# An RWKV-6 recurrence with a gated feed-forward behind it: x of one superblock transposed by DMA, products moved to GpSimd, and a new order

## The chip, the core and the metric

One NeuronCore of a Trainium2 chip runs the whole kernel. Its engines work side by side, each through a queue of its own in order: TensorE (PE; PEld is its weight loading), VectorE (DVE), ScalarE (ACT), GpSimd (POOL) and SyncE (SP), which here only issues transfers. An instruction waits at the head of its queue until the semaphores that it needs have come, and what stands behind it waits too. PE writes its results to PSUM; the other data lie in SBUF.

The metric is the device time of one execution in microseconds (us). Three runs of the kernel before gave 204.59, 204.86 and 205.42; the median is 204.86.

## The reference, cut to what matters

```python
def _attn_ref(r, k, v, w, u):              # batch 4, heads 8, positions 768, head size 48
    for t in range(S):
        cur = einsum('bhd,bhe->bhde', u[None] * kt, vt)
        y[:, :, t] = einsum('bhd,bhde->bhe', rt, state + cur)
        state = wt[:, :, :, None] * state + einsum('bhd,bhe->bhde', kt, vt)

def _moe_ref(x, w_gate, w_val, w_out, rms_g):   # 3072 rows of 384, inner size 1536
    xn = x / sqrt(mean(x * x, axis=-1) + 1e-06) * rms_g
    g = xn @ w_gate
    return (g * (1.0 / (1.0 + exp(-g))) * (xn @ w_val)) @ w_out
```

The first function carries a state of 48 x 48 for each batch and head along the positions. Its output, with the heads side by side, is the x of the second.

## The kernel before, in words

The 768 positions are cut into six superblocks n = 0 to 5 of 128 positions, and each holds the four batches j = 0 to 3. For one (n, j) the recurrence is done in chunk form:

- `load_k`, `load_r`, `load_v`, `load_w` fetch the inputs (SP). `ln` takes the logarithm of w (ACT); `cs_mm` sums it along the positions on PE; `cs_add` makes k's sums out of r's on DVE; `exp_r` and `exp_k` are the exponentials (ACT).
- `r_mul` (L438) and `k_mul` (L444) multiply r and k with them into `rk`. For (n, j) in `EXPR_SB` the exponential of r's sums is written to a tile `er` in SBUF, else over the sums in PSUM. `K_POOL` lists the k products that GpSimd computes; it reads SBUF, so their exponential is written to `ek`.
- `rk` is transposed: for superblocks 0 and 1 on PE (`rk_pe`, L467) with a copy on ACT (`rk_tr`, L476), from 2 on by a DMA transpose (`rk_tr`, L472).
- `q_mm` forms the scores (L485, L487), `q_mask_e`, `q_copy_o` and `q_mask_o` (L503, an affine select on POOL) mask them, `y_mm` (L530, L533) gives the output. `st_mm` (L513) and `st_new` bring the state on.
- `bonus_mul` (two POOL products, L450 and L451), `bonus_sum` and `bonus_v` make the term with u; `x_add` adds it.
- `x_sq` and `x_rstd` give the scale of each row, `xn_mul` (L556) applies it. x is then transposed into `xnt[n]`: for superblocks 0 to 3 on PE (`xn_pe`, L567) and copied out by DVE with the factor rms_g (`xn_out`, L578); for 4 and 5 by a DMA transpose (`xn_tr`, L561), and DVE multiplies rms_g in afterwards (`xn_gain`, L582) in three pieces of 128 features, each over all 512 rows.

The feed-forward of a superblock has 12 gate blocks and 12 value blocks of three matmuls (`gate_mm`, `val_mm`, L593), each followed by `silu` on ACT or `h_mul` on DVE, and four output blocks of 12 matmuls (`o_mm`, L625). A block needs all four batches of `xnt[n]`. `load_gv` and `load_wo` fetch the weights, and POOL issues them (L344, L350): a small and a large piece of each of w_gate and w_val (columns 0 to 511 and 512 to 1535), and three pieces of w_out.

Which step comes when is written out by hand in the string `ORDER`; every engine's queue takes its part of it in that order. So the feed-forward of superblock n is interleaved with the recurrence of n + 1. `warm` is a matmul whose result nobody reads. PSUM has eight banks in three rings: two for r's sums and gate blocks ("a"), two for k's sums and value blocks ("b"), four for the rest ("q").

The lines of the recurrence's two products and of the gain, and how a step is called:

```python
nc.vector.tensor_tensor(out=rk[:, n % 2, j, 0, :, 0:D], in0=inp["r", n, j],
                        in1=bank["cs_r", n, j][:, NP:NP + DM]..., op=ALU.mult)
eng = nc.gpsimd if (n, j) in K_POOL else nc.vector
for step in ORDER.split():
    fn, n, j = step.split(".")
    fns[fn](int(n), int(j))
```

Of the kernel before, what the change touches and what calls it, by code (L numbers as in the profile page):

```python
# [12 lines left out]
ALU = mybir.AluOpType  # L13
# [22 lines left out]
cast_v.0.2 cs_mm.1.0 exp_r.1.0 exp_k.1.0 bonus_sum.0.2 q_mask_o.0.0 q_mm.0.1 q_mask_e.0.1 q_mask_o.0.1 bonus_mul.0.3
bonus_sum.0.3 bonus_v.0.0 rk_pe.0.3 rk_tr.0.3 cs_mm.1.1 exp_k.1.1 exp_r.1.1 cast_v.0.3 load_v.2.1 load_k.2.1 load_r.2.3
load_r.2.2 load_k.2.0 warm.14.0 y_mm.0.0 warm.19.0 x_add.0.0 warm.3.0 x_sq.0.0 cast_v.1.0 q_mm.0.2 q_mask_e.0.2
q_mask_o.0.2 x_rstd.0.0 xn_mul.0.0 q_mm.0.3 y_mm.0.1 warm.35.0 x_add.0.1 warm.34.0 x_sq.0.1 x_rstd.0.1 load_v.2.0
q_mask_e.0.3 w_tot.0.3 load_gv.0.0 y_mm.0.2 bonus_v.0.2 x_add.0.2 x_sq.0.2 st_mm.0.3 cs_mm.1.3 xn_mul.0.1 x_rstd.0.2  # L40
load_k.2.2 q_mask_o.0.3 y_mm.0.3 w_tot.1.0 k_mul.1.0 bonus_v.0.3 x_add.0.3 x_sq.0.3 r_mul.1.0 st_mm.0.2 xn_pe.0.1
xn_out.0.1 xn_pe.0.0 load_gv.0.1 xn_out.0.0 st_new.0.3 cs_mm.1.2 xn_mul.0.2 xn_pe.0.2 st_mm.0.1 xn_out.0.2 st_new.0.1
x_rstd.0.3 xn_mul.0.3 xn_pe.0.3 xn_out.0.3 bonus_mul.1.0 load_gv.1.0 exp_r.1.3 exp_k.1.2 exp_r.1.2 rk_pe.1.0 rk_tr.1.0
r_mul.1.1 st_mm.1.0 st_new.1.0 w_tot.1.1 bonus_sum.1.0 bonus_mul.1.1 exp_k.1.3 gate_mm.0.1 gate_mm.0.0 silu.0.1
q_mm.1.0 q_mask_e.1.0 w_tot.1.3 val_mm.0.0 val_mm.0.1 k_mul.1.1 rk_pe.1.1 st_new.0.2 silu.0.0 h_mul.0.0 r_mul.1.3
rk_tr.1.1 gate_mm.0.3 silu.0.3 h_mul.0.1 load_gv.1.1 bonus_v.1.0 gate_mm.0.2 silu.0.2 q_copy_o.1.0 val_mm.0.2
gate_mm.0.4 silu.0.4 val_mm.0.3 q_mm.1.1 h_mul.0.2 gate_mm.0.6 silu.0.6 q_copy_o.1.1 k_mul.1.3 h_mul.0.3 q_mask_o.1.0
w_tot.1.2 y_mm.1.0 x_add.1.0 gate_mm.0.8 rk_pe.1.3 gate_mm.0.5 q_mask_e.1.1 bonus_sum.1.1 silu.0.8 val_mm.0.4 h_mul.0.4
k_mul.1.2 r_mul.1.2 bonus_mul.1.3 x_sq.1.0 rk_tr.1.3 silu.0.5 gate_mm.0.11 val_mm.0.5 val_mm.0.9 h_mul.0.5 q_mask_o.1.1
gate_mm.0.9 cast_v.1.1 st_mm.1.1 st_new.1.1 silu.0.9 h_mul.0.9 rk_pe.1.2 rk_tr.1.2 val_mm.0.6 h_mul.0.6 gate_mm.0.7  # L50
q_mm.1.2 q_mask_e.1.2 silu.0.11 q_copy_o.1.2 q_mm.1.3 q_mask_e.1.3 load_wo.1.0 x_rstd.1.0 load_wo.0.0 val_mm.0.11
h_mul.0.11 q_copy_o.1.3 val_mm.0.8 h_mul.0.8 load_wo.2.0 bonus_v.1.1 silu.0.7 xn_mul.1.0 y_mm.1.1 x_add.1.1
gate_mm.0.10 silu.0.10 x_sq.1.1 bonus_sum.1.3 val_mm.0.7 h_mul.0.7 val_mm.0.10 h_mul.0.10 o_mm.0.0 bonus_mul.1.2
bonus_sum.1.2 o_out.0.0 bonus_v.1.3 cast_v.1.3 q_mask_o.1.3 y_mm.1.3 x_add.1.3 ln.2.0 cs_mm.2.0 cs_add.2.0 q_mask_o.1.2
cast_v.1.2 y_mm.1.2 xn_pe.1.0 xn_out.1.0 st_mm.1.3 ln.2.1 cs_mm.2.1 x_rstd.1.1 xn_mul.1.1 exp_k.2.0 exp_r.2.0
bonus_v.1.2 x_add.1.2 x_sq.1.2 x_sq.1.3 load_v.2.2 x_rstd.1.2 cs_add.2.1 exp_r.2.1 w_tot.2.0 st_new.1.3 ln.2.2 o_mm.0.1
ln.2.3 x_rstd.1.3 xn_mul.1.3 st_mm.1.2 st_new.1.2 xn_mul.1.2 w_tot.2.1 r_mul.2.0 o_out.0.1 cast_v.2.1 bonus_mul.2.1
# [75 lines left out]
def kernel(  # L133
# [41 lines left out]
    def sel(s):  # L175
        return {(int(x[0]), int(x[1])) for x in s.split()}
# [501 lines left out]
```

## Time and profile before

| What | Value |
|---|---|
| median of three runs | 204.86 us |
| the profiled execution's own time | 204.97 us |
| span, first to last instruction | 203.3 us |
| mean granted clock of TensorE | 0.999 |
| transfers | 32.41 MB, mean 159 GB/s |

A row of the timeline gives start, duration, engine, line of the kernel, operation, output and inputs, shape and count; in brackets the idle time before it and what ended that. A row of a group gives count, total busy time, mean duration in ns, idle time before and its causes. In the rows of windows the busy time of PE, PEld, DVE, ACT and POOL follows the length. A row of issues ends with the median time from issue to landing.

### The profile page before, as it was taken

To read this page: it belongs to the slowest core of one execution; us is meant where nothing else is said; L and a number is where in the kernel's file an instruction comes from. 1 tells how busy PE (TensorE), PEld (TensorE's weight loads), DVE (VectorE), ACT (ScalarE), POOL (GpSimd) and SP (SyncE) were. 2 spreads that over 40 slices of the span, in tenths; PEclk is the share of its full clock that TensorE was granted. 3 is DMA by queue.
4 is the path that set the end of the run, shared out by engine and by line. 5 is a ranking of instruction groups with operands and counts; after the bars stand their busy time and mean duration, and the time that the engine had idled before them with its cause. 6 is when DMAs were issued, how large, how long until landed. Compare 5 with 4: busy or idle time off the path is not lost.

```text
span 203.3 us, 4409 instructions
## 1 busy us (share of the span) xinstructions
PE 189.9 (93%) x1569; PEld 113.1 (56%) x1588; DVE 154.2 (76%) x299; ACT 137.7 (68%) x278; POOL 125.4 (62%) x186
## 2 busy tenths in 40 slices
PE   1999879998999999999999999999969999999994
PEld 1566555554666555665556665555635565555562
DVE  6158999889899879997899998687996685145621
ACT  2379999767899647998659886688975666154300
POOL 6079983592659968999978789776895543000000
PEclk9999999999999999999999999999999999999999
DMA  6998999999986999995999999997155201121012
GB/s 156 266 224 177 187 220 208 212 175 215 203 172 141 204 161 206 248 234 128 204 171 221 241 215 207 221 194 165 44 141 159 61 23 40 58 77 42 0 64 92
DMA packets 121566, 32.41 MB, mean 159 GB/s; under 512 B 116420, under 2 KB 120392, under 8 KB 121544
## 3 DMA queue, kind: packets, MB, share of 16 engines
q1 hardware_dynamic: 119504, 28.58, 66.1%
q0 software_dynamic: 2032, 3.54, 9.6%
q8 instruction: 12, 0.20, 0.4%
q14 instruction: 10, 0.08, 0.1%
q10 hardware_dynamic: 8, 0.00, 0.0%
HBM read 25.96 MB, written 4.72 MB: 151 GB/s over the span
## 4 chain that ended last, share of the span: by engine, by line
PE 84%; ACT 6%; DVE 3%; issue 2%; POOL 1%; DMA 1%; POOLq 0%; DVEq 0%
PE ps_bv L593 12%; PE ps_au L593 12%; PE ps_av L593 10%; PE ps_bu L593 10%; PE ps_qu L625 7%; PE ps_qx L625 5%; PE ps_qv L625 4%; PE ps_qz L625 4%; PE ps_qx L367 1%; DVE rk L438 1%; ACT xn L556 1%; ACT junk L543 1%; DMA xnt<-xn 1%; PE ps_qv L485 1%; PE ps_qu L467 1%
## 5 line engine op out<-in xcount | busy, mean ns | idle before, releaser
L625 PEld LDWEIGHTS <-ht 128*128 128x128 bf16 x300 | 28.4, 98 | 17.0
L593 PEld LDWEIGHTS <-wv_sb 128*128 128x128 bf16 x216 | 23.2, 114 | 21.2 <-issue 1.5
L230 ACT ACTIVATE sg<-ps_au 128x512 bf16<-128x512 f32 x38 | 22.8, 599 | 17.4 <-PE ps_au L593 13.9
L593 PEld LDWEIGHTS <-wg_sb 128*128 128x128 bf16 x216 | 23.1, 114 | 18.9 <-issue 0.2
L611 DVE TENSOR_TENSOR ht<-ps_bv,sg 128x512 bf16<-128x512 f32 x38 | 26.1, 688 | 9.3 <-PE ps_bv L593 5.1
L230 ACT ACTIVATE sg<-ps_av 128x512 bf16<-128x512 f32 x34 | 20.4, 600 | 16.1 <-PE ps_av L593 9.7
L593 PE MATMUL ps_bv<-xnt,wv_sb 128*128 128x512 bf16 x110 | 30.7, 380 | 0.3
L593 PE MATMUL ps_au<-xnt,wg_sb 128*128 128x512 bf16 x110 | 30.5, 380 | 0.4
L611 DVE TENSOR_TENSOR ht<-ps_bu,sg 128x512 bf16<-128x512 f32 x34 | 23.3, 686 | 9.2 <-ACT sg L230 6.0
L450 POOL TENSOR_TENSOR ruk<-rt,kt 128x384 f32<-128x384 f32 x24 | 24.6, 1023 | 7.8 <-DMA rt<-in_r_dram 7.0
L593 PE MATMUL ps_bu<-xnt,wv_sb 128*128 128x512 bf16 x94 | 27.1, 380 | 2.0 <-DVE xnt L582 1.5
L460 POOL TENSOR_TENSOR ydiag<-vt,diag 128x384 f32<-128x384 f32 x24 | 20.1, 840 | 12.1 <-DVE diag L455 12.0
L593 PE MATMUL ps_av<-xnt,wg_sb 128*128 128x512 bf16 x99 | 27.3, 380 | 0.1
L451 POOL TENSOR_TENSOR ruk<-ruk,u_bc 128x384 f32<-128x384 f32 x24 | 24.2, 1009 | 1.9
L503 POOL TENSOR_SCALAR_AFFINE_SELECT qts<-qts 128x512 bf16<-128x512 bf16 x20 | 12.6, 637 | 8.8 <-ACT qts L496 7.3
L556 ACT ACTIVATE xn<-xb,rstd 128x384 bf16<-128x384 f32 x24 | 14.5, 611 | 4.5 <-POOL rstd L552 4.3
L625 PE MATMUL ps_qu<-wo_sb,ht 128*128 128x384 bf16 x96 | 16.9, 326 | 0.0
L444 POOL TENSOR_TENSOR rk<-kt,ek 128x384 bf16<-128x384 f32 x16 | 15.9, 1001 | 1.1 <-ACT ek L230 1.1
L228 ACT ACT_TABLE_LOAD x10 | 12.8, 1283 | 1.8 <-PEq L662 1.6
L543 ACT ACTIVATE junk<-xb 128x384 bf16<-128x384 f32 x24 | 12.4, 518 | 1.3 <-DVE xb L538 1.1
L230 ACT ACTIVATE lw<-wt 128x384 bf16<-128x384 f32 (+1 forms) x20 | 11.0, 578 | 2.8 <-DMA wt<-in_w_dram 2.7
L455 DVE TENSOR_REDUCE diag<-ruk 128x8 f32<-128x384 f32 x24 | 12.8, 545 | 0.0
(156 smaller groups left out, 370.8 us busy)
## 6 DMA issues: line engine op xcount, KB each, us to landing
kt<-in_k_dram SPq DMA_DIRECT2D x24, 192.0 KB, 3.6
vt<-in_v_dram SPq DMA_DIRECT2D x24, 192.0 KB, 4.1
rt<-in_r_dram SPq DMA_DIRECT2D x24, 192.0 KB, 3.9
out_dram<-ob SPq DMA_DIRECT2D x23, 192.0 KB, 2.8
wt<-in_w_dram SPq DMA_DIRECT2D x16, 192.0 KB, 3.6
wt<-in_w_dram SPq DMA_DIRECT2D x4, 384.0 KB, 4.4
wo_sb<-in_moe_w_out_dram POOLq DMA_DIRECT2D x3, 384.0 KB, 7.1
wg_sb<-in_moe_w_gate_dram POOLq DMA_DIRECT2D x1, 768.0 KB, 9.4
```

Of the source, the lines that this page charges most:

```text
L228: nc.scalar.preload_act_table_set(table_name)
L230: return nc.scalar.activation(**kw).ins
L444: eng.tensor_tensor(out=rk[:, n % 2, j, 1, :, 0:D], in0=inp["k", n, j], in1=bank["cs_k", n, j][:, 0:DM].rearrange("p (h d) -> p h d", h=H) ...
L450: nc.gpsimd.tensor_tensor(out=ruk[n, j], in0=inp["r", n, j], in1=inp["k", n, j], op=ALU.mult)
L451: nc.gpsimd.tensor_tensor(out=ruk[n, j], in0=ruk[n, j], in1=u_bc, op=ALU.mult)
L455: nc.vector.tensor_reduce(out=diag[n, j].rearrange("p h o -> p (h o)"), in_=ruk[n, j], axis=mybir.AxisListType.X, op=ALU.add)
L460: nc.gpsimd.tensor_tensor(out=ydiag[n, j], in0=inp["v", n, j], in1=diag[n, j].to_broadcast([128, H, D]), op=ALU.mult)
L543: nc.scalar.activation(out=junk, in_=xb[n, j], func=AF.Square, accum_out=rstd[n, j][:, 0:1])
L556: nc.scalar.activation(out=xn, in_=xb[n, j], func=AF.Copy, scale=rstd[n, j][:, 1:2])
L593: nc.tensor.matmul(ps, lhsT=units(ws, c, f), rhs=xnt[n][:, c, :], start=(c == 0), stop=(c == KC - 1))
L611: nc.vector.tensor_tensor(out=ht[n][:, f, :], in0=bank.pop(("v", n, f)), in1=bank.pop(("sg", n, f)), op=ALU.mult)
L625: nc.tensor.matmul(ps[:, cols], lhsT=ht[n][:, f, b * L:(b + 1) * L], rhs=wo_sb[:, f, cols], start=(f == 0), stop=(f == FC - 1))
```

## The change

The transposes of x of superblock 3 move from PE to DMA. For superblocks 3 to 5 rms_g is multiplied in on GpSimd, in four pieces (one for each batch, all 384 features) instead of DVE's three. k's products of superblock 1 move from DVE to GpSimd. The exponential of r's sums of superblock 1 stays in PSUM. The warm matmuls read a tile `zero` of their own, 128 x 128, and there are 48 of them and not 36. `ORDER` is a new one throughout; the parts below are those up to the first block of the feed-forward, the end of superblock 2's feed-forward and the end of superblock 3's.

```diff
 ORDER = """
...
+load_k.0.0 load_w.0.1 warm.18.0 warm.5.0 warm.17.0 load_w.0.0 load_r.0.2 warm.10.0 warm.36.0 warm.21.0 ln.0.1 warm.1.0
+warm.14.0 load_r.0.0 bonus_mul.0.0 bonus_sum.0.0 load_w.0.3 load_v.0.0 load_w.0.2 load_k.0.1 load_r.0.1 bonus_mul.0.1
+ln.0.0 cs_mm.0.0 warm.33.0 load_v.0.1 load_k.0.2 bonus_mul.0.2 cs_mm.0.1 warm.11.0 warm.24.0 warm.26.0 warm.37.0
+warm.25.0 warm.29.0 warm.2.0 warm.19.0 load_k.0.3 load_r.0.3 exp_r.0.0 w_tot.0.0 r_mul.0.0 load_v.0.2 load_r.1.1
+load_v.1.0 load_r.1.0 load_k.1.0 load_v.0.3 load_k.1.1 load_r.1.3 load_r.1.2 load_k.1.3 exp_r.0.1 exp_k.0.0 k_mul.0.0
...
+xn_pe.0.1 xn_out.0.1 xn_mul.0.2 xn_pe.0.2 warm.45.0 xn_out.0.2 x_rstd.0.3 xn_mul.0.3 xn_pe.0.3 xn_out.0.3 rk_pe.1.1
+rk_tr.1.0 bonus_sum.1.0 bonus_v.1.0 bonus_mul.1.3 exp_r.1.2 r_mul.1.2 w_tot.1.3 st_mm.1.0 exp_k.1.2 q_mm.1.0
+q_copy_o.1.0 q_mask_o.1.0 bonus_mul.1.1 k_mul.1.2 val_mm.0.3 val_mm.0.1 w_tot.1.2 gate_mm.0.1 silu.0.1 st_new.1.0
...
+y_mm.3.2 x_add.3.2 val_mm.2.9 h_mul.2.9 h_mul.2.11 ln.4.0 cs_mm.4.0 ln.4.1 cs_mm.4.1 cs_add.4.1 bonus_mul.4.1
+cs_add.4.0 x_sq.3.1 x_rstd.3.1 x_sq.3.2 x_sq.3.3 x_rstd.3.3 o_mm.2.2 o_out.2.2 o_mm.2.1 xn_mul.3.1 xn_tr.3.1 exp_r.4.1
+w_tot.4.1 o_mm.2.0 st_new.3.3 bonus_sum.4.1 r_mul.4.1 exp_r.4.0 w_tot.4.0 r_mul.4.0 xn_mul.3.3 xn_tr.3.3 ln.4.3
+cs_mm.4.3 xn_gain.3.0 x_rstd.3.2 exp_k.4.0 k_mul.4.0 xn_mul.3.2 xn_tr.3.2 cs_add.4.3 exp_k.4.1 k_mul.4.1 st_mm.4.1
...
+w_tot.4.3 r_mul.4.3 exp_k.4.3 st_mm.4.0 st_new.4.0 st_new.4.1 o_mm.2.3 o_out.2.3 out_dma.2.3 xn_gain.3.1 xn_gain.3.3
+load_k.5.0 xn_gain.3.2 gate_mm.3.0 val_mm.3.1 val_mm.3.0 silu.3.0 k_mul.4.2 gate_mm.3.4 gate_mm.3.3 bonus_mul.4.3
...
+val_mm.3.5 h_mul.3.5 st_mm.4.2 y_mm.4.3 gate_mm.3.11 cs_mm.5.1 silu.3.11 val_mm.3.11 x_add.4.3 x_sq.4.3 x_rstd.4.1
+xn_mul.4.1 x_rstd.4.2 xn_mul.4.2 h_mul.3.11 x_rstd.4.3 load_v.5.0 load_v.5.3 cast_v.5.3 xn_tr.4.0 load_r.5.1
...
 """
...
-    EXPR_SB = sel("10 11 12 13")
-    K_POOL = sel("20 21 22 23 30 31 32 33 40 41 42 43 50 51 52 53")
+    EXPR_SB = sel("")
+    K_POOL = sel("10 11 12 13 20 21 22 23 30 31 32 33 40 41 42 43 50 51 52 53")
...
+    GAIN_POOL = (3, 4, 5)
...
     junk = const.tile([128, DM], BF16)
-    nc.vector.memset(junk, 0.0)
+    zero = const.tile([128, 128], BF16)
+    nc.vector.memset(zero, 0.0)
...
     def warm(n, j):
         ps = psum("q", ("warm", n, j), [128, DM])
-        nc.tensor.matmul(ps, lhsT=junk[:, 0:128], rhs=junk, start=True, stop=True)
+        nc.tensor.matmul(ps.rearrange("p (a x) -> p a x", a=3), lhsT=zero, rhs=bc_mid(zero, 3), start=True, stop=True)
...
     def xn_gain(n, c):
-        nc.vector.tensor_scalar(out=xnt[n][:, c, :], in0=xnt[n][:, c, :], scalar1=gT[:, c:c + 1],
-                                scalar2=None, op0=ALU.mult)
+        if n in GAIN_POOL:
+            x = xnt[n][:, :, c * L:(c + 1) * L]
+            nc.gpsimd.tensor_tensor(out=x, in0=x, in1=gT.to_broadcast([128, KC, L]), op=ALU.mult)
+        else:
+            nc.vector.tensor_scalar(out=xnt[n][:, c, :], in0=xnt[n][:, c, :], scalar1=gT[:, c:c + 1],
+                                    scalar2=None, op0=ALU.mult)
```

More of the change, by code (lines that the diff above doesn't have):

```diff
@@ L36 @@
[L36 to L45, printed above, removed]
```

181 lines of the change are left out of this document (88 added, 93 removed).

## The prediction

> **What bounds the kernel now.** First I read the page's busy shares and the chain that ended last.
>
> ```profile
> span 203.3 us, 4409 instructions
> PE 189.9 (93%) x1569; PEld 113.1 (56%) x1588; DVE 154.2 (76%) x299; ACT 137.7 (68%) x278; POOL 125.4 (62%) x186
> ...
> PE 84%; ACT 6%; DVE 3%; issue 2%; POOL 1%; DMA 1%; POOLq 0%; DVEq 0%
> ```
>
> TensorE (PE) is busy for 93% of the span and carries 84% of the chain, so time is lost only where PE stands still or does what it need not. Next, the timeline of PE from the first block of the feed-forward on.
>
> ```profile
> 31.57 0.81 PE L593 MATMUL ps_au<-xnt,wg_sb 128*128 128x512 bf16 x2
> ...
> 44.90 0.33 PE L513 MATMUL ps_qz<-vb,rk 128*128 128x96 bf16 x4
> 46.47 0.62 PE L467 MATMUL ps_qx<-ident,rk 128*128 128x128 bf16 x8 [1.24 <-DVE rk L438]
> ...
> 122.08 0.81 PE L593 MATMUL ps_au<-xnt,wg_sb 128*128 128x512 bf16 x3
> 122.72 0.81 PE L593 MATMUL ps_bv<-xnt,wv_sb 128*128 128x512 bf16 x3
> ...
> 146.68 2.11 PE L625 MATMUL ps_qu<-wo_sb,ht 128*128 128x384 bf16 x12
> 149.07 0.41 PE L593 MATMUL ps_bu<-xnt,wv_sb 128*128 128x512 bf16 x1 [0.27 <-DVE xnt L582]
> 150.74 0.38 PE L593 MATMUL ps_bu<-xnt,wv_sb 128*128 128x512 bf16 x1 [1.26 <-DVE xnt L582]
> ```
>
> A gate or value block (three matmuls) takes 122.72 - 122.08 = 0.65 us from start to start, its printed 0.81 less the 0.16 by which ends overlap; an output block so takes 1.95, a state block of four 0.17. At 44.90 PE is free at 45.07 and resumes at 46.47: **1.4 us** lost to r's product of superblock 1. The output block of 146.68 is through at 148.63; one matmul of 0.22 fits in before 150.74: **1.9 us** lost on the rms_g products of superblock 4. These are the only large holes from 31.57 on, so the end is set by three things: when the first block starts, how much PE work is left then, and the holes.
>
> **Work taken off PE.** Twelve transposes of x (three for each of four batches) go.
>
> ```profile
> 60.49 0.33 PE L567 MATMUL ps_qu<-ident,xn 128*128 128x128 bf16 x3
> 60.69 0.34 PE L404 MATMUL ps_av<-lw,mask_lt 128*128 128x384 bf16 x1
> ...
> 32.96 0.23 PE L485 MATMUL ps_qv<-rkT 48*128 48x128 bf16 x1
> ...
> 33.29 0.84 PE L593 MATMUL ps_bv<-xnt,wv_sb 128*128 128x512 bf16 x3
> ```
>
> Three take 60.69 - 60.49 = 0.20 at most: 4 x 0.18 = **-0.7**, since they stand in PE's own line between output blocks. The new order also puts rk_pe.1.1 (eight transposes of 0.06) and q_mm.1.0 (33.29 - 32.96 = 0.33) ahead of the first block, and two state blocks (2 x 0.17) behind it: **-0.45** of work left then. The 12 more warm matmuls all stand before the first block, where PE is not the limit; their new operand only keeps them apart from ScalarE's squares, and I take both at nothing.
>
> **Superblock 1.** r's product reads PSUM, k's goes to GpSimd (POOL).
>
> ```profile
> 44.28 2.13 DVE L438 TENSOR_TENSOR rk<-rt,er 128x384 bf16<-128x384 f32 x1
> ...
> L438 DVE TENSOR_TENSOR rk<-rt,ps_av 128x384 bf16<-128x384 f32 x10 | 5.5, 548 | 0.0
> L444 DVE TENSOR_TENSOR rk<-kt,ek 128x384 bf16<-128x384 f32 x4 | 3.2, 808 | 0.0
> L444 POOL TENSOR_TENSOR rk<-kt,ek 128x384 bf16<-128x384 f32 x16 | 15.9, 1001 | 1.1 <-ACT ek L230 1.1
> L582 DVE TENSOR_SCALAR xnt<-xnt,gT 128x512 bf16<-128x512 bf16 x6 | 3.6, 655 | 3.7 <-DMA xnt<-xn 3.5 <-issue 0.2
> L460 POOL TENSOR_TENSOR ydiag<-vt,diag 128x384 f32<-128x384 f32 x24 | 20.1, 840 | 12.1 <-DVE diag L455 12.0
> ```
>
> The product that held PE took 2.13; from PSUM it takes 0.548 on average, and VectorE (DVE) is rid of four k products of 0.81 as well. The first hole goes: **-1.4**. The PSUM bank of r's sums is held longer, but all four products stand before the first gate block, which would want it: nothing.
>
> **Where the first block starts.** Up to it ScalarE (ACT) has the full queue.
>
> ```profile
> 10.09 0.85 PE L389 MATMUL ps_au<-lw,mw 128*128 128x384 bf16 x2
> ...
> 11.17 0.48 ACT L230 ACTIVATE ps_au<-ps_au 128x388 f32<-128x388 f32 x1 [3.81 <-PE ps_au L393]
> ...
> 30.34 0.47 ACT L230 ACTIVATE er<-ps_au 128x388 f32<-128x388 f32 x1
> 30.71 0.48 ACT L230 ACTIVATE ek<-ps_bv 128x384 f32<-128x384 f32 x1
> ...
> 31.46 1.02 ACT L476 COPY rkT<-ps_qu 128x1024 bf16<-128x1024 bf16 x1
> ```
>
> ScalarE waits 3.81 for the first sums, which stand behind 13 warm matmuls. In the new order 8 stand there, so it starts about 1.5 sooner; but its next instruction is now the second batch's exponential, for whose sums it waits again until about 11.3, and only some 0.3 is gained. Before the last xn_mul of superblock 0 it has two more exponentials of 30.71 - 30.34 = 0.37: that xn_mul, which ends where the row of 30.34 begins, will end near 30.8. Then the new order has rk_tr.1.0 (0.9 of its 1.02 before the next can begin) and q_mm.1.0 (0.33) ahead of the first block: 32.1 to 32.2, against 31.57: **+0.6**, bounds -0.5 (the second wait vanishes) and +1.6 (one more wait of 1 us in that queue).
>
> **Weights behind GpSimd's queue.** POOL issues the weight loads, in its own order.
>
> ```profile
> 15.38 1.00 POOL L450 TENSOR_TENSOR ruk<-rt,kt 128x384 f32<-128x384 f32 x1 [0.42 <-DMA rt<-in_r_dram]
> 16.46 1.00 POOL L451 TENSOR_TENSOR ruk<-ruk,u_bc 128x384 f32<-128x384 f32 x1
> ...
> 21.01 0.98 POOL L344 DMA_DIRECT2D wg_sb<-in_moe_w_gate_dram  x1
> ...
> 26.57 0.80 POOL L344 DMA_DIRECT2D wg_sb<-in_moe_w_gate_dram  x1
> ...
> 30.45 0.80 POOL L344 DMA_DIRECT2D wv_sb<-in_moe_w_val_dram  x1
> ...
> wv_sb<-in_moe_w_val_dram POOLq DMA_DIRECT2D x1, 768.0 KB, 9.8
> wg_sb<-in_moe_w_gate_dram POOLq DMA_DIRECT2D x1, 384.0 KB, 6.0
> ```
>
> The bonus product at 15.38 waited for the twelfth load of the order. The second one will wait for the tenth, which by that should land near 13.7. From there POOL has three bonus pairs of 2 x 1.08, four v products of 0.8, two k products of 1.0, two issues of 0.8 and about 1.2 of waiting for the first exponential of superblock 1: 13.7 + 6.5 + 3.2 + 2.0 + 1.6 + 1.2 = 28.2 at the issue of the large gate load (26.57 now). The small gate load comes 1.8 before that, at 26.4 against 21.01: it lands at 32.4 or later (6.0), wanted at 32.2 + 2 x 0.65 = 33.5. One more issue, pair and k product put the large value load at 32.2 (30.45 now): it lands at 42.0 (9.8), wanted after ten blocks and 3.6 of attention, at 42.3. Both just arrive: **+0.4** (0 to 1.2, POOL's wait of 1.2 made twice as long). The last w_out load, behind a wait for v of superblock 1, is of the same kind: **+0.3** (0 to 1.3, which is two thirds of an output block, the matmuls that do not need it yet).
>
> **GpSimd in superblocks 2 to 4.** This is the price of the change.
>
> ```profile
> 82.56:121.09 38.53, 38.20 (x343) 23.70 (x343) 35.07 (x74) 31.03 (x66) 33.71 (x50) 1.00 0.97 205
> 121.09:149.07 27.98, 27.50 (x218) 15.98 (x221) 22.95 (x43) 21.90 (x46) 22.05 (x33) 1.00 0.75 165
> ...
> rkT<-rk SPq DMA_TRANSPOSE x16, 2.9
> ...
> xnt<-xn SPq DMA_TRANSPOSE x8, 2.3
> ```
>
> The windows run from the first output block of superblock 1 to the first block of 3, and on to that of 4; after the length stand PE, weight loads, DVE, ACT, POOL. A gain on POOL is new to the trace: 384 elements with one broadcast operand, nearest to L460, so 0.85 (no less than the 0.65 of L582, which has VectorE's pace, no more than the 1.0 of L444). The new order's queue in the first window is that of now plus four gains (3.4): 37.1 of POOL against 38.5 - 0.7 = 37.8 of PE. POOL enters about 1 us ahead, as its first instruction wants a square done earlier. Of its 4.8 of pauses now most are waits for PE, which shrink as POOL falls behind. Walking both queues, q_mask_o.3.0 and q_mask_o.3.3 end 0.2 each after y_mm wants them. After y_mm.3.2, ScalarE (two squares, three xn_mul, four exponentials and logarithms) ends the last xn_mul at 5.6, POOL the k products of 4.0 and 4.1 at 7.2, the last transpose lands at 8.0, three gains end at 9.9; PE has 9.85 of work there and 0.1 to 0.9 more to wait. Together **+0.9** (0, or 3.5 if every pause is kept: 37.1 + 4.8 - 1 lies 3.1 above 37.8, and 0.4 for the handover). SyncE (SP) holds at the three transposes, and behind them rk_tr.4.1, rk_tr.4.0 and superblock 5's loads: these two start near 7.4 and land by 10.5 (2.9), wanted at 13.7; nothing.
>
> In superblock 3's blocks POOL reaches q_mask_o.4.2 some 0.3 late: **+0.4** (0 to 1). At its end each gain now follows its own transpose. Counted from y_mm.4.3, ScalarE has a silu, a square, two xn_mul, a table load of 1.3, an exponential and the last xn_mul: 5.1; that transpose lands at 7.4, POOL's gains end at 9.0; PE has three blocks, four output blocks and four sums, 10.4. The second hole closes: **-1.9**. For superblock 5 the same walk leaves 2 us. Two more table loads (ln.5.1 among the silus) are 2 x 1.28 for an engine with 15 of work in 19: **+0.2** (0 to 1).
>
> ```profile
> L228 ACT ACT_TABLE_LOAD x10 | 12.8, 1283 | 1.8 <-PEq L662 1.6
> ```
>
> The Trainium skill, page "GPSIMD Engine Reference", section "4.1 Engine selection", gives elementwise work to VectorE and calls GpSimd about twice as slow with two inputs. This case's k products, 1001 against 548 to 808, agree in part. A gain at twice L582's 0.655 would be 1.3, an estimate that adds 1.8 in the first window and brings the sum to about 205.
>
> **Sum.** -0.7 - 0.45 - 1.4 - 1.9 + 0.6 + 0.4 + 0.3 + 0.9 + 0.4 + 0.2 = -1.65. The profiled execution took 204.97 (203.3 of span and 1.7 around it), 0.11 above the median of the runs: 203.3 by it, **203.2** for the median.
>
> **The rivals.**
>
> *A load that starves (slower).* The 24th load of the order meets the weights:
>
> ```profile
> 23.71 3.25 SPq L243 DMA_DIRECT2D rt<-in_r_dram  x1
> ...
> DMA to landing us min/median/max: 2.9/3.9/13.7
> ```
>
> It lands 13.7 after its issue, at 37.4. In the new order the 24th is k.1.3, and POOL's product of it stands before the last weight issue. Against: with weights first issued near 24, not 21, it should land by 31. From about 31.2 on each microsecond is lost: at 37.4 the value load is issued at 38.5 and lands between 45 and 48, 2.5 to 5.5 after it is wanted: 206.9, bounds 205.2 to 208.5. The Trainium skill, page "Trainium Kernel Development and Optimization", section "Key Constraints", says that loads issued from several engines run on the same 16 DMA engines and interleave; the 13.7 beside a median of 3.9 agrees.
>
> *GpSimd becomes the bound.* Its pauses stay and 3.5 stands for the 0.9: 205.8. For it: 37.1 of 37.8. Against: the pauses follow PE.
>
> *Slack takes everything.* No new hole at all: 203.2 less the last five terms, 2.2: 201.0. For it: only two waits cost PE anything now.
>
> *Superblock 1 is not cured.* rk_pe.1.3 waits for POOL's k product, queued behind bonus pairs, where it waited for VectorE: the 1.4 stays, 204.6.
>
> **Chances.** Forecast 0.42, its own range 202.0 to 204.4; starved load 0.15; GpSimd 0.15; slack 0.13; not cured 0.15. The measurement can't tell less than 0.5%, 1.0 us, from no change: faster lies below 203.8, slower above 205.9. Faster: 0.36 of the forecast, 0.13 of slack, 0.03 of GpSimd: 0.52. Slower: 0.13 of the load, 0.12 of GpSimd: 0.25. The remaining 0.23 is the same. The range 200.9 to 206.9 leaves out the far half of the starved load and a few hundredths at either end.
>
> **What would show it.** The first block near 32.2; no wait of L467 for VectorE in superblock 1; POOL without long pauses from the first output block of superblock 1 on, PE waits of 0.2 to 0.6 named after its mask or gain; no hole before superblock 4. It is wrong if POOL waits for k before its last weight issue, if the first block starts after 33.5, or if PE waits over 1 us for a mask or a gain.

## The result, and the profile after

| | before | after |
|---|---|---|
| median of 15 runs each, side by side | 204.59 us | 203.20 us |
| lowest and highest run | 203.54, 205.42 | 202.33, 204.53 |
| ratio, with its 95% interval | | 0.9944 [0.9923, 0.9965] |
| span of the profiled execution | 203.3 us | 201.5 us |

The kernel is 0.56% faster, and the time is the predicted one. In the experiments below seven runs took over 1.5% longer than the fastest of their kernel; the medians count them, the ratios leave them out. The page's busy shares and chain of after:

```profile
span 201.5 us, 4430 instructions
PE 191.4 (95%) x1588; PEld 113.4 (56%) x1588; DVE 144.8 (72%) x285; ACT 139.5 (69%) x280; POOL 137.6 (68%) x202
...
PE 79%; DMA 9%; ACT 4%; POOL 3%; issue 2%; DVE 1%; POOLq 0%; ACTq 0%; DVEq 0%
```

VectorE lost 9.4 us of work (154.2 to 144.8) and GpSimd gained 12.2. TensorE's busy time rose by 1.5 although 12 transposes went: 12 short warm matmuls are new, and before's trace lacks 19 matmul records (1569 beside 1588 weight loads). So this row does not say where the time came from. The timeline of TensorE does (line numbers are 2 to 6 higher than before: L441 is L438 there, L470 is L467, L599 is L593, L631 is L625; in the experiments they shift by one or two more):

```profile
32.35 0.84 PE L599 MATMUL ps_bv<-xnt,wv_sb 128*128 128x512 bf16 x3
...
34.05 0.84 PE L599 MATMUL ps_av<-xnt,wg_sb 128*128 128x512 bf16 x3 [0.21 <-DMA wg_sb<-in_moe_w_gate_dram]
...
41.96 0.61 PE L470 MATMUL ps_qu<-ident,rk 128*128 128x128 bf16 x8
...
54.32 0.81 PE L631 MATMUL ps_qx<-wo_sb,ht 128*128 128x384 bf16 x4 [0.27 <-DMA wo_sb<-in_moe_w_out_dram]
...
118.14 2.11 PE L631 MATMUL ps_qz<-wo_sb,ht 128*128 128x384 bf16 x12
120.13 0.81 PE L599 MATMUL ps_au<-xnt,wg_sb 128*128 128x512 bf16 x3
...
143.44 0.32 PE L407 MATMUL ps_au<-lw,mask_lt 128*128 128x384 bf16 x1 [0.18 <-ACT lw L232]
...
145.87 2.11 PE L631 MATMUL ps_qx<-wo_sb,ht 128*128 128x384 bf16 x12
148.44 0.81 PE L599 MATMUL ps_av<-xnt,wg_sb 128*128 128x512 bf16 x3 [0.46 <-POOL xnt L587]
```

Read from the top. The first block starts at 32.35. The first gate block follows two value blocks, of which the second starts at 33.03, and should start at 33.68; it starts 0.37 later, for weights. The transposes of rk in superblock 1 (41.96 is the last) have no wait in front; the hole of 1.4 is gone. At 54.32 an output block, eight matmuls old, waits for w_out (0.27 by the row, 0.43 with the gap that it leaves in the sequence). At 118.14 the last output block of superblock 2 starts, and 1.99 later the first block of superblock 3: GpSimd's four new gains cost TensorE nothing. From 145.87 an output block runs to 147.82, and the first block of superblock 4 starts at 148.44: 0.6 is what is left of the second hole.

### The profile page after: what moved, and what is told of

The parts are those of the page before. It is cut to its first block, busy times and chain, and to the rows that moved or that the text cites. A ratio compares the mean times of both kernels' runs of the same rounds, so it can differ in the third digit from the quotient of the medians.

```text
span 201.5 us, 4430 instructions
## 1 busy us (share of the span) xinstructions
PE 191.4 (95%) x1588; PEld 113.4 (56%) x1588; DVE 144.8 (72%) x285; ACT 139.5 (69%) x280; POOL 137.6 (68%) x202
## 4 chain that ended last, share of the span: by engine, by line
PE 79%; DMA 9%; ACT 4%; POOL 3%; issue 2%; DVE 1%; POOLq 0%; ACTq 0%; DVEq 0%
PE ps_av L599 11%; PE ps_au L599 11%; PE ps_bv L599 10%; PE ps_bu L599 9%; PE ps_qz L631 6%; PE ps_qv L631 6%; PE ps_qx L631 4%; DMA wg_sb<-in_moe_w_gate_dram 4%; DMA wo_sb<-in_moe_w_out_dram 3%; PE ps_qu L631 2%; DMA xnt<-xn 2%; PE ps_qu L488 1%; ACT L230 1%; PE ps_qv L370 1%; PE ps_qz L370 1%
## 5 line engine op out<-in xcount | busy, mean ns | idle before, releaser
L631 PEld LDWEIGHTS <-ht 128*128 128x128 bf16 x300 | 28.5, 98 | 18.1 <-issue 0.9
L599 PEld LDWEIGHTS <-wg_sb 128*128 128x128 bf16 x216 | 23.2, 114 | 21.0 <-DMA wg_sb<-in_moe_w_gate_dram 0.7
L617 DVE TENSOR_TENSOR ht<-ps_bv,sg 128x512 bf16<-128x512 f32 x37 | 25.4, 687 | 11.2 <-ACT sg L232 6.3
L599 PEld LDWEIGHTS <-wv_sb 128*128 128x128 bf16 x216 | 22.7, 114 | 17.8 <-issue 0.2
L232 ACT ACTIVATE sg<-ps_au 128x512 bf16<-128x512 f32 x36 | 21.5, 598 | 15.3 <-PE ps_au L599 12.0
L232 ACT ACTIVATE sg<-ps_av 128x512 bf16<-128x512 f32 x36 | 21.5, 597 | 14.5 <-PE ps_av L599 11.5
L599 PE MATMUL ps_bv<-xnt,wv_sb 128*128 128x512 bf16 x111 | 30.2, 380 | 0.0
L599 PE MATMUL ps_av<-xnt,wg_sb 128*128 128x512 bf16 x108 | 29.3, 380 | 0.7 <-POOL xnt L587 0.5
L599 PE MATMUL ps_au<-xnt,wg_sb 128*128 128x512 bf16 x108 | 29.3, 380 | 0.0
L599 PE MATMUL ps_bu<-xnt,wv_sb 128*128 128x512 bf16 x105 | 28.4, 379 | 0.0
L617 DVE TENSOR_TENSOR ht<-ps_bu,sg 128x512 bf16<-128x512 f32 x35 | 24.0, 685 | 6.1 <-PE ps_bu L599 3.4
L447 POOL TENSOR_TENSOR rk<-kt,ek 128x384 bf16<-128x384 f32 x20 | 19.9, 1001 | 2.6 <-ACT ek L232 2.3
L631 PE MATMUL ps_qz<-wo_sb,ht 128*128 128x384 bf16 (+1 forms) x96 | 15.9, 316 | 0.0
L631 PE MATMUL ps_qv<-wo_sb,ht 128*128 128x384 bf16 x84 | 14.8, 326 | 0.0
```

Of the source, the lines that this page charges most:

```text
L232: return nc.scalar.activation(**kw).ins
L447: eng.tensor_tensor(out=rk[:, n % 2, j, 1, :, 0:D], in0=inp["k", n, j], in1=bank["cs_k", n, j][:, 0:DM].rearrange("p (h d) -> p h d", h=H) ...
L599: nc.tensor.matmul(ps, lhsT=units(ws, c, f), rhs=xnt[n][:, c, :], start=(c == 0), stop=(c == KC - 1))
L617: nc.vector.tensor_tensor(out=ht[n][:, f, :], in0=bank.pop(("v", n, f)), in1=bank.pop(("sg", n, f)), op=ALU.mult)
L631: nc.tensor.matmul(ps[:, cols], lhsT=ht[n][:, f, b * L:(b + 1) * L], rhs=wo_sb[:, f, cols], start=(f == 0), stop=(f == FC - 1))
```

## The experiments

Besides the change itself twelve kernels were run. Ratios are to runs of the kernel before, made beside each of them.

| kernel | median us | ratio, 95% |
|---|---|---|
| after | 203.20 | 0.9944 [0.9923, 0.9965] |
| after, r's product of 1 from SBUF | 204.50 | 0.9997 [0.9974, 1.002] |
| after, gains on VectorE | 215.86 | 1.0555 [1.0513, 1.0597] |
| after, x of 3 by TensorE | 207.47 | 1.0146 [1.0094, 1.0199] |
| after, k products of 1 on VectorE | 210.07 | 1.0274 [1.0231, 1.0317] |
| the same, three of them placed later | 213.10 | 1.0397 [1.0374, 1.0421] |
| after, 12 warm matmuls fewer | 203.94 | 0.9961 [0.9938, 0.9984] |
| after, weights issued sooner | 209.55 | 1.0248 [1.021, 1.0285] |
| after, two waits mended | 203.43 | 0.9950 [0.9923, 0.9977] |
| before, k products of 1 on GpSimd | 204.27 | 0.9954 [0.9924, 0.9983] |
| before, gains on GpSimd | 225.28 | 1.0994 [1.0965, 1.1023] |
| before, k products and gains of 4 on GpSimd | 209.80 | 1.0267 [1.0226, 1.0308] |
| the same, bonus product in its old place | 204.68 | 0.9967 [0.9927, 1.0007] |

### r's product reads SBUF again

```diff
-    EXPR_SB = sel("")
+    EXPR_SB = sel("10 11 12 13")
```

> The kernel after, with r's product of superblock 1 reading the exponential from SBUF again (one line of the code; the order stays). Theory (the holes of the kernel before add up one by one, and reading PSUM closed the first of them): the four r products stretch from about 0.55 to between 0.9 and 2.1 us wherever a GpSimd operation runs beside them, and TensorE waits for VectorE ahead of a rank-48 transpose of superblock 1 again, 0.5 to 1.4 us in all: 203.7 to 204.6. Rival A (the gain is only the shorter list of TensorE): TensorE's list is untouched, 203.2. Rival B (only the new order counts, the parts do not): the order is untouched, 203.2, and the products may be long without TensorE waiting for them.

The whole gain is gone. But TensorE does not wait ahead of a transpose of rk in its blocks; the loss stands before the first block, which starts at 34.57 and not at 32.35 in the profiled run. VectorE's timeline of this run, then GpSimd's, then windows of TensorE (length, busy time and count, granted clock, DMA share, GB/s):

```profile
22.55 0.97 DVE L437 TENSOR_TENSOR wcol<-er,half_of 128x8 f32<-128x8 f32 x1
23.44 0.54 DVE L441 TENSOR_TENSOR rk<-rt,er 128x384 bf16<-128x384 f32 x1
...
25.11 1.81 DVE L441 TENSOR_TENSOR rk<-rt,er 128x384 bf16<-128x384 f32 x1
```

```profile
22.49 1.00 POOL L447 TENSOR_TENSOR rk<-kt,ek 128x384 bf16<-128x384 f32 x1 [1.26 <-ACT ek L232]
23.43 0.98 POOL L347 DMA_DIRECT2D wv_sb<-in_moe_w_val_dram  x1
24.45 1.63 POOL L463 TENSOR_TENSOR ydiag<-vt,diag 128x384 f32<-128x384 f32 x2
```

```profile
25.00:30.00 5.00, 3.51 (x48) 1.00 1.18 204
30.00:35.00 5.00, 4.80 (x43) 0.66 1.18 205
```

The same product takes 0.54 while GpSimd issues a load and 1.81 while GpSimd multiplies; even the product of 8 columns takes 0.97 beside a k product (0.16 from PSUM). That the port is what they share is said by the Trainium skill, page "SBUF — State Buffer", section "SBUF: two separate sides": a VectorE operation with two SBUF inputs and a GpSimd operation that reads SBUF shut each other out for a whole instruction. The rows agree.

In this profile the loss has a second part. Against after, TensorE is 1.39 late at 29.10, and 2.22 late at the first block, without a longer wait between: the granted clock fell. But the profiled run (205.05, mean clock 0.992) is the only one of the twelve in which it fell. The other eleven have a mean clock of 0.999 or 1.0, and their median is 204.48. So the 1.3 that the median lost are the long products, as in the 1.39 at 29.10, and not the clock. More on the clock with the warm matmuls.

### The k products of superblock 1, taken away and alone

```diff
-    K_POOL = sel("10 11 12 13 20 21 ...")
+    K_POOL = sel("20 21 ...")
```

> The kernel after, with the four k products of superblock 1 on VectorE again. Theory: this part carries none of the gain by itself. VectorE has four products of 0.8 more and GpSimd four of 1.0 fewer, so that the weight loads behind them are issued 2 to 4 us sooner and the waits for weights (0.2 to 0.4 us) shrink: 202.6 to 203.4. Rival A and rival B: 203.2. A further rival, that VectorE's queue is what held the transposes of superblock 1: a wait of TensorE for VectorE of 0.5 to 1.5 comes back, 203.7 to 204.7.

Far worse than any of these: the first block starts at 37.42, and not for VectorE's load. VectorE's timeline, and TensorE's:

```profile
22.56 0.56 DVE L447 TENSOR_TENSOR rk<-kt,ek 128x384 bf16<-128x384 f32 x1 [3.65 <-ACT ek L232]
```

```profile
24.10 0.40 PE L470 MATMUL ps_qv<-ident,rk 128*128 128x128 bf16 x4 [2.24 <-DVE rk L447]
```

The product waits 3.65 for its exponential at the head of VectorE's queue; a k product of superblock 0 stands behind it, and TensorE waits for that one. The order was made for a product that waits on another engine. So three of the four were put later:

> The kernel after with the k products of superblock 1 on VectorE, as in the run that took 210.1, but three of them moved behind the work they held up there: in that run k's product of batch 0 waited 3.65 for its exponential at the head of VectorE's queue, and masks, sums and a product of superblock 0 stood behind it. If it was that wait at the head of an in-order queue, most of the 6.9 comes back: 203.2 to 205. If VectorE's load itself is the reason (four products of 0.55 to 0.87 more in the stage that sets the first block), it stays above 206.

213.10: neither expectation. The wait at 22.56 is gone, the first block starts at 33.69, and something else is late, on VectorE:

```profile
41.86 0.76 DVE L447 TENSOR_TENSOR rk<-kt,ek 128x384 bf16<-128x384 f32 x1 [7.56 <-DMA kt<-in_k_dram]
```

Two loads of k of superblock 1 are the culprits. By the order, the product at 41.86 is that of batch 2, whose load lands as its wait ends; GpSimd waits until just before, 41.21, for the load of batch 3, which landed 16.5 after its issue. That is the longest landing of k here, against 6.4 in after (last row of the view of the tile kt from 18 to 45, of this run and of after):

```profile
DMA to landing us min/median/max: 3.5/5.4/16.5
```

```profile
DMA to landing us min/median/max: 3.8/4.1/6.4
```

This is the load that starves, the rival with a chance of 0.15. Without four k products in its queue GpSimd issues the weights sooner: the large gate load directly behind the small one of 25.70, the large value load at 29.32, against 27.93 and 31.73. A later kernel tests that alone.

The opposite edit, on the kernel before:

```diff
-    K_POOL = sel("20 21 ...")
+    K_POOL = sel("10 11 12 13 20 21 ...")
```

> The kernel before, with the four k products of superblock 1 on GpSimd and nothing else of the change. First theory: worth nothing by itself, between -0.5 and +0.5 of 204.5, since TensorE waited for r's product and not for k's. Second theory (a part needs its order): in the old order the products stand ahead of GpSimd's weight loads and bonus products without their places having been made for it; the first block starts 0 to 1 later or the last weights come late: 204.5 to 206.5.

The ratio, 0.9954, some 0.9 us, is more than the first theory allowed (0.5, which its interval reaches) and the opposite of the second. It cannot be told from that of the whole change. The profile is of one of its fastest runs (202.63). TensorE's timeline where the first hole was, and VectorE's:

```profile
45.06 0.33 PE L513 MATMUL ps_qz<-vb,rk 128*128 128x96 bf16 x4
45.23 0.61 PE L467 MATMUL ps_qx<-ident,rk 128*128 128x128 bf16 x8
```

```profile
43.35 0.55 DVE L438 TENSOR_TENSOR rk<-rt,er 128x384 bf16<-128x384 f32 x1
```

The hole is closed, with r's product still reading SBUF. In the kernel before a k product stood in front of it on VectorE:

```profile
43.18 1.17 DVE L444 TENSOR_TENSOR rk<-kt,ek 128x384 bf16<-128x384 f32 x1
44.28 2.13 DVE L438 TENSOR_TENSOR rk<-rt,er 128x384 bf16<-128x384 f32 x1
```

It pushed r's product into the GpSimd products from 44.12 on. Without it r's product is over at 43.90, before GpSimd's next product at 44.94, and takes 0.55. So one line of the change closes the first hole, in the old order, in this profile. Its runs spread more, though (202.54 to 206.45), than those of after.

### Weights issued sooner

```diff
-... exp_k.1.0 k_mul.1.0 exp_r.1.0 rk_tr.0.2 load_gv.0.1 ... bonus_v.0.2 k_mul.0.3
+... exp_k.1.0 load_gv.0.1 k_mul.1.0 load_gv.0.0 exp_r.1.0 rk_tr.0.2 ... bonus_v.0.2 load_gv.1.0 k_mul.0.3
...
-... load_gv.0.0 k_mul.1.1 load_gv.1.0 ... load_gv.1.1
+... k_mul.1.1 load_gv.1.1 ...
```

> The kernel after with the four loads of gate and value weights issued sooner on GpSimd's queue: the two small ones on either side of the first k product of superblock 1, the first large one ahead of superblock 0's last ydiag, the last behind the second k product; by the trace of after some 1 to 3 us sooner each. Theory, from the run that took 213.1 (there a load of k landed 16.5 after its issue and TensorE waited 7.8): what the k products on GpSimd do is to hold the weight loads back; with the weights ahead, a late load of superblock 1 lands 12 to 17 after its issue instead of at most 6.4, the k product on GpSimd and TensorE behind it wait 3 to 8 for it: 206 to 213. Rival (the loads share the engines and nothing starves; the wait for the gate weights of 0.4 goes): 202.6 to 203.2.

209.55, as the theory has it. GpSimd's timeline and the view of the tile kt from 18 to 45:

```profile
28.07 0.80 POOL L346 DMA_DIRECT2D wv_sb<-in_moe_w_val_dram  x1
...
39.72 0.99 POOL L446 TENSOR_TENSOR rk<-kt,ek 128x384 bf16<-128x384 f32 x1 [8.73 <-DMA kt<-in_k_dram]
```

```profile
DMA to landing us min/median/max: 3.5/3.6/16.1
```

The last large load goes out at 28.07 and not 31.73, the wait of 0.37 for weights is gone, and a k load of superblock 1 lands 16.1 after its issue. GpSimd waits 8.73, and TensorE behind it:

```profile
40.77 0.61 PE L469 MATMUL ps_qv<-ident,rk 128*128 128x128 bf16 x4 [3.83 <-POOL rk L446]
41.85 1.47 PE L598 MATMUL ps_au<-xnt,wg_sb 128*128 128x512 bf16 x3
```

The four blocks from 41.85 take 1.27 each from start to start instead of 0.65: another 2.5 lost after the wait is over, in this profile. One of the four runs has a mean clock of 1.0 and took 209.15, hardly less than the others; where it lost its time no trace shows.

### Twelve warm matmuls fewer

```diff
-... warm.22.0 ... warm.39.0 ... warm.35.0 warm.40.0 ... warm.41.0 warm.34.0 ... warm.42.0 ... warm.43.0 ... warm.44.0 warm.46.0 warm.47.0 ... warm.45.0
```

> The kernel after without the last 12 of its 48 warm matmuls on zeros (nothing of the computation is left out). In the prediction the 12 additional ones counted for nothing. Theory that they do count: with the r products slowed, TensorE was busy for 3.5 of the 5 us from 25 to 30, and the granted clock fell to 0.66 in the 5 us behind it; in the kernel after, TensorE is busy there for 4.05, of which some 1.8 are these matmuls. Without them the clock should fall for some 3 us around the first blocks, for 1 to 1.7 longer: 204.2 to 205. Rival (they only fill time in which nothing else could run): 203.2, with a granted clock of 1.0 from 25 to 40; or 202.8, if they held up real work.

The windows of this run, and of after:

```profile
25.00:30.00 5.00, 3.11 (x54) 1.00 1.15 197
30.00:35.00 5.00, 4.19 (x31) 0.66 1.18 205
```

```profile
25.00:30.00 5.00, 4.05 (x62) 1.00 1.15 206
30.00:35.00 5.00, 4.25 (x46) 1.00 1.19 208
```

The clock falls where it was expected to, and the end of TensorE's work is 1.15 later in this profile. It falls in every run: all twelve have a mean clock of 0.983 to 0.992, and the fifteen of after 0.997 or more. The ratio is 0.0017 above after's, some 0.35 us, and the two intervals overlap: the mechanism is shown, its price differs from run to run. The five runs with 0.983 took 204.06 to 205.87, the seven with 0.990 to 0.992 took 202.73 to 204.34, and only the latter are like after. In the profiled run with r from SBUF it was the same: busy for 62 to 70% of these 5 us, TensorE runs at about half rate for some 3 us behind them; at 81% it does not. The Trainium skill, page "TensorE: Matmul & The Clock Gate", gives as a rule that gaps over some 3.4 us bring the clock down (section "HAM oscillation — how this bites in real kernels"), and reports short idling that does so in one kernel (section "A second HAM failure mode: psum-queue depth-cycling"). The longest wait ahead of the fall was 1.1 here, so the rows go against the rule and with the report.

### x of superblock 3 by TensorE again

```diff
-... xn_tr.3.0 ... xn_gain.3.0 ... xn_gain.3.1 xn_gain.3.3 xn_gain.3.2
+... xn_pe.3.0 xn_out.3.0 ...
-    GAIN_POOL = (3, 4, 5)
+    GAIN_POOL = (4, 5)
```

> The kernel after, with x of superblock 1 (the third of the order to be treated otherwise, the one whose x the change moved to the DMA) transposed by TensorE and copied out of PSUM again. Theory: 12 transposes of 0.06 stand in TensorE's line again and no transfer is waited for there: 0.5 to 0.9 longer, 203.7 to 204.1, without a new wait. Rival A (the whole gain of 1.1 to 1.4 is the shorter list of TensorE): 204.3 to 204.6, the time before. Rival B (order alone): 203.2.

(The text names superblock 1; the kernel puts back x of superblock 3.) The three transposes of one batch put TensorE 0.17 further behind after (from 0.36 to 0.53 at 117.8), so 0.7 for four, as predicted. Then a wait that the expectation had not:

```profile
122.19 1.14 PE L631 MATMUL ps_qv<-wo_sb,ht 128*128 128x384 bf16 x6 [2.62 <-DVE xnt L581]
```

The output block takes the PSUM bank of the last batch's transposes, and VectorE copies them out only at 121.58, behind products of superblock 4 that wait for their exponentials. In after no bank has to be emptied there. So the price of the transposes alone is read from the profile, not from the median.

### The gains on VectorE in the new order, on GpSimd in the old one

```diff
-    GAIN_POOL = (3, 4, 5)
+    GAIN_POOL = ()
```

In `ORDER` the three pieces stand behind the last transpose of each superblock.

> The kernel after, with the rms_g products of superblocks 3 to 5 on VectorE again, in three pieces of 512 behind the last transpose of each superblock. Theory: the hole ahead of superblock 4's first block comes back, since the first piece waits for the last transpose and the two others follow at 0.65 us: 1 to 2 us longer, 204.2 to 205.2, nearly all of it ahead of superblock 4; GpSimd, freed of 12 operations of 0.83, gives nothing back. Rival A (shorter list): 203.2. Rival B (order alone): 203.2. A further rival, that GpSimd's 10 us more work cost TensorE something in superblocks 2 to 4: 202.2 to 203.0.

And on the kernel before, `xn_gain` of 4 and 5 as in the change, each step directly behind its own transpose:

```diff
-... xn_tr.4.0 x_sq.4.1 x_rstd.4.1 xn_mul.4.1 ... xn_tr.4.1 ... xn_gain.4.0 ... xn_gain.4.2 xn_gain.4.1
+... xn_tr.4.0 xn_gain.4.0 x_sq.4.1 x_rstd.4.1 xn_mul.4.1 ... xn_tr.4.1 xn_gain.4.1 ... xn_tr.4.3 xn_gain.4.3
```

> The kernel before, with the rms_g products of superblocks 4 and 5 on GpSimd, one for each batch, each directly behind its own transpose; nothing else of the change. First theory (the holes are separate, each part is worth its own hole): the wait of 1.9 ahead of superblock 4's second gate block goes to between 0 and 0.6, GpSimd's 7 operations of 0.83 cost TensorE nothing: 202.6 to 203.8, and the trace shows the other holes as before. Second theory, formed on the first four runs (a part is worth something only in an order that is made for it; each engine takes its work in order, so a piece that waits holds all behind it): the gains hold GpSimd's queue at each transpose, k products and masks behind them come late, and the time is 204.5 or more. Rival A (only TensorE's list counts): 204.6, as before.

Both are far off every number. The first waits 2.77 and 0.59 for gains of superblock 3, which stand behind other products on VectorE, and 4.13 for a state that VectorE has queued behind a gain; each time half rate follows. TensorE's timeline there:

```profile
123.86 0.41 PE L598 MATMUL ps_au<-xnt,wg_sb 128*128 128x512 bf16 x1 [2.77 <-DVE xnt L588]
124.86 0.85 PE L598 MATMUL ps_au<-xnt,wg_sb 128*128 128x512 bf16 x2 [0.59 <-DVE xnt L588]
125.51 1.49 PE L598 MATMUL ps_bu<-xnt,wv_sb 128*128 128x512 bf16 x3
...
153.96 4.00 PE L630 MATMUL ps_qv<-wo_sb,ht 128*128 128x384 bf16 x12 [4.13 <-DVE st L522]
```

The second loses it on GpSimd:

```profile
140.70 0.83 POOL L583 TENSOR_TENSOR xnt<-xnt,gT 128x384 bf16<-128x384 bf16 x1 [3.81 <-DMA xnt<-xn]
141.61 0.19 POOL L551 TENSOR_SCALAR rstd<-rstd 128x1 f32<-128x1 f32 x1
...
145.47 0.83 POOL L583 TENSOR_TENSOR xnt<-xnt,gT 128x384 bf16<-128x384 bf16 x1 [3.03 <-DMA xnt<-xn]
```

A gain waits for its transpose, the rstd of the next batch stands behind it, and without that rstd the next transpose cannot start: four batches that overlapped now go one after the other.

In a place made for them the gains do close the hole. On the kernel with k products on GpSimd, behind the last rstd:

```diff
-... xn_tr.4.3 exp_k.5.0 exp_r.5.1 r_mul.5.1 ln.5.2 ln.5.3 bonus_mul.5.3 bonus_sum.5.3 ... xn_gain.4.0 cast_v.5.0 ... xn_gain.4.2 xn_gain.4.1
+... xn_tr.4.3 xn_gain.4.0 xn_gain.4.1 cast_v.5.0 xn_gain.4.2 exp_k.5.0 exp_r.5.1 xn_gain.4.3 r_mul.5.1 ... bonus_v.5.2 bonus_mul.5.3 ... bonus_sum.5.3 bonus_v.5.3
```

> The kernel before with k's products of superblock 1 on GpSimd (the run that took 204.27, ratio 0.9954), and now also the rms_g products of superblock 4 on GpSimd, one for each batch, but placed behind the last rstd of superblock 4, so that no rstd stands behind a gain that waits for a transpose; the bonus pair 5.3 goes behind the k products. Theory (a gain in a place made for it closes the hole): the wait of 1.0 ahead of superblock 4's second gate block goes to 0 to 0.4 and nothing replaces it: 0.6 to 1.2 less than with the k products alone, ratio 0.988 to 0.993, 202.2 to 203.3. Rival (GpSimd, with 5.4 us of work put ahead of the first gate block, is late with the fourth gain or with the k products behind it): no better than the k products alone, ratio 0.995 to 1.000.

No second hole follows superblock 4's first block, but a new wait stands further on:

```profile
150.55 0.81 PE L595 MATMUL ps_bu<-xnt,wv_sb 128*128 128x512 bf16 x3 [0.48 <-POOL xnt L582]
...
165.06 0.20 PE L531 MATMUL ps_qu<-vb,qts 128*128 128x48 bf16 x1 [3.88 <-DVE qts L490]
```

VectorE held a mask behind the sum of a bonus product that GpSimd, its own queue halted by the moved sum, had not made. With the bonus product where it was:

> As the run before it with k products and superblock 4's gains on GpSimd (209.8, where the hole ahead of superblock 4 closed and a wait of 3.9 for a bonus product came in its place), but the bonus product 5.3 keeps its place: it now stands between the second and the third gain, in time in which GpSimd waited for a transpose, and its sum on VectorE stands behind the two cumulative sums it would hold up. Theory (what took the gain away there was the bonus pair behind the k products, not GpSimd's load): no wait over 1 for GpSimd or VectorE from superblock 4's first block on, the hole of 1.0 becomes 0.2 to 0.8 ahead of the first block: 0.2 to 0.7 less than with the k products alone, ratio to before 0.991 to 0.996, 202.7 to 203.7. Rival (3.3 us of gains ahead of superblock 5's k products are too much for GpSimd there): their transposes land late, TensorE waits 1 or more for a product of superblock 5, ratio 0.998 or above.

```profile
148.16 0.81 PE L595 MATMUL ps_bu<-xnt,wv_sb 128*128 128x512 bf16 x3 [0.61 <-POOL xnt L582]
```

The row answers to these of the kernel without the gains:

```profile
147.03 0.38 PE L593 MATMUL ps_bu<-xnt,wv_sb 128*128 128x512 bf16 x1
148.42 0.59 PE L593 MATMUL ps_bu<-xnt,wv_sb 128*128 128x512 bf16 x2 [1.02 <-DVE xnt L582]
```

The hole is 0.61 with the gains on GpSimd, 1.02 with them on VectorE: 0.4 smaller. But superblock 5's transposes come 0.8 late (a wait ahead of its scores), and the ratio, 0.9967, is no better than with the k products alone.

### Two waits mended

```diff
+... load_wo.0.0 load_wo.2.0 ...
-... exp_r.5.1 xn_mul.4.3 ln.5.2 ...
+... xn_mul.4.3 ln.5.2 exp_r.5.1 ...
```

> The kernel after with two steps moved: the last w_out load is issued directly behind the first pair, and in superblock 4's end the exponential 5.1 goes behind the last xn_mul, so that this xn_mul does not wait for the table load in between. The trace of after has three waits there: 0.43 for w_out, 0.63 for the last gain ahead of superblock 4, 0.35 for a logarithm of superblock 5. Theory (they are separate): 0.4 to 1.2 less than after, ratio to before 0.988 to 0.993, 202.2 to 203.3. Rival (every step moved ahead holds up another in its queue, as in the runs of call one): 203.2 or more, ratio 0.994 and above, with a new wait of TensorE or of GpSimd in the trace.

In its profile the waits for w_out and for superblock 4's last gain are gone, a new one of 0.16 for an r product stands at 146.33, and 0.6 is won from 34.80 to the end. But the wait for the first gate weights is longer in that execution, though nothing ahead of it was touched:

```profile
34.80 0.84 PE L599 MATMUL ps_av<-xnt,wg_sb 128*128 128x512 bf16 x3 [0.71 <-DMA wg_sb<-in_moe_w_gate_dram]
```

The median is that of after, and the ratio lies where the rival had it. Whether the longer wait is the spread of the weights' landing stays open.

## Why the prediction was right

The sum was -1.65; TensorE's last instruction ends at 198.2 instead of 200.3 in the profiles, -2.0, and the medians differ by 1.4. Right in total, and in part by errors that cancel. That 203.20 was met to the hundredth is luck: the forecast started from 204.86, and the kernel before took 204.59 this time.

| term | predicted | trace of after |
|---|---|---|
| transposes; work moved ahead of the first block | -0.7; -0.45 | -0.7 by the profile of the run that undid it; -0.4 |
| first hole | -1.4 | -1.4 |
| second hole | -1.9 | -1.3 |
| first block | +0.6 | +0.8 |
| gate weights, w_out | +0.4, +0.3 | +0.4, +0.4 |
| GpSimd in 2 to 4 | +0.9, +0.4 | 0 |
| table loads | +0.2 | +0.35 |

The last column adds up to -1.9. The -0.4 is `rk_pe.1.1` (31.21 to 31.65) and `q_mm.1.0` (32.02 to 32.35) ahead of the first block, less the two state blocks behind it (34.72 to 35.06).

*First block.* It starts at 32.35. The last xn_mul ends where ScalarE's next row begins, at 30.88, 0.1 later than in the walk; from there to the scores at 32.02 it took 1.14, and the walk had 0.9 for the copy.

*First hole.* The size held; the step that credited it to reading PSUM failed. With the k products alone on GpSimd the old order has no such hole, with r's product in SBUF; nor has the new order with r's product in SBUF. Reading PSUM alone, in the old order, was not run. In the new order it pays before the first block: 1.3 us, by the run that undid it.

*Second hole.* The walk took 2.3 us from the last xn_mul to the landed transpose, the median of the view of transfers. That xn_mul ends at 142.98. SyncE's timeline, and GpSimd's with the gain that the landing releases:

```profile
142.73 0.57 SPq L646 DMA_DIRECT2D out_dram<-ob  x1
143.39 1.18 SPq L564 DMA_TRANSPOSE xnt<-xn  x1
```

```profile
147.57 0.83 POOL L587 TENSOR_TENSOR xnt<-xnt,gT 128x384 bf16<-128x384 bf16 x1 [1.98 <-DMA xnt<-xn]
```

The issue waits 0.4 for an output store in SyncE's queue, and the transfer lands about 147.5, 4.1 after its issue: 4.5 instead of 2.3, which is more than the 0.6 that is left of the hole. Why this one took 4.1 is not shown.

*GpSimd.* A gain takes 0.826, as bounded (0.85), and not 1.3. The estimate of 1.3 doubled the 0.655 of a piece of 512 columns, and a gain has 384. Over the 1536 columns of a superblock, four gains take 3.30 on GpSimd, 1.7 times the 1.97 that three pieces took on VectorE with one tensor as input. So the trace does not contradict the factor of about two of the Trainium skill (page "GPSIMD Engine Reference", section "4.1 Engine selection"). The oversized term is the queue. The window from superblock 1's first output block to superblock 3's first block (PE, PEld, DVE, ACT, POOL after the length):

```profile
81.83:120.13 38.30, 38.30 (x337) 23.35 (x336) 32.72 (x69) 30.89 (x65) 35.49 (x51) 1.00 0.90 185
```

It holds 35.49 of GpSimd's work, not 37.1: the new order has three ydiag products, a cast and an rstd fewer in it, and one k product and one bonus pair more; the walk kept the old list. By their mean durations these make about half of the 1.6; the rest is not attributed. So no mask and no gain came late, and the 1.3 set aside for it was not spent.

*Warm matmuls at nothing.* This step failed. They keep the clock up ahead of the first block: without 12 of them it is granted at 0.66 on average over 5 us in the profile, and falls in all twelve runs.

*The load that starves.* It did not hit k, with less room than the chance of 0.15 said. The argument against it, that the weights go out later, is right, and what makes them late is the k products themselves: they are GpSimd's delay line. Other loads starve in after too. A load of w takes 15.8 to land and one of v 13.7, and TensorE does not wait for them; the view of the tile wt of after:

```profile
DMA to landing us min/median/max: 3.1/4.0/15.8
```

So sooner weights do not make the slow loads; they make k one of them. Weights some 2 to 4 us sooner bring 209.55, above the rival's 206.9; in the profile half rate follows the wait.

*GpSimd as the bound, superblock 1 not cured* fell: GpSimd's window above has 2.8 to spare, and TensorE has no wait at its transposes. *Slack takes everything* did not hold either: waits of 0.2 to 0.6 stayed.

## What to carry to other kernels

In a kernel with hand-ordered queues a part of a change has no price of its own: undone in an order made for it, each of the four parts here cost 1.3 to 12.7 us, and one of them alone, in the old order, gave a gain that cannot be told from that of the whole change. The new order with none of the parts was not run. Ask of each moved instruction what it will wait for and what then stands behind it, and test a part alone in both orders. A product that is moved to the queue which issues loads also sets when these loads go out; and a wait on TensorE can cost more than its length, by a lower clock behind it.

## What had not been expected of the hardware

- TensorE's granted clock fell to about half for some 3 us after 5 us in which it was busy for 62% or 70%, with no wait above 1.1; at 81% it stayed. With 12 warm matmuls fewer it fell in twelve runs of twelve, with r from SBUF in one of twelve, and why not in the other eleven no trace shows. After a wait of 3.83 four blocks took 1.27 instead of 0.65 each; after a wait of 2.62 in another run they kept their pace. Whether the length of a wait decides is open.
- Beside 2.3 MB of weights some input loads land 13 to 18 after their issue in every profile here (13.9 in before, 15.8 in after), against a median of about 4. With weights 2 to 4 us sooner it was a load of k that was wanted soon (16.1).
- The same VectorE product of 384 columns took 0.54 or 1.81 from SBUF, by what GpSimd did meanwhile, and 0.54 to 0.55 from PSUM.
